# The first batch's keys pooled by matmuls place by place, two rows of inverse sums made by TensorE, and w_out's column scale from sums of magnitudes

## The chip, the cores and the metric

The kernel runs on one core of one Trainium2 chip. The metric is the device time of one execution in microseconds, taken as the median of several. "Before" is the kernel as it stands, "the change" the kernel with the edits below. Besides the five engines (TensorE, VectorE, ScalarE, GpSimd, SyncE; in the profile PE, DVE, ACT, POOL, SP) the core has 16 DMA engines, here fed from SyncE's queue alone.

## What is computed

```python
B, S, C, F = 4, 12288, 128, 2048
kv_pool = kv.reshape(B, 96, 4, 8, 4, C).mean(axis=(2, 4))      # 768 keys a batch, 16 places each
k = v = kv_pool.reshape(B, 768, C) @ w_sr
a = softmax(q @ k.T / sqrt(C))
x = (a @ v).reshape(-1, C)
h = x @ w_in
out = (h - tanh(h)) @ w_out
```

Inputs and output are float32, and the weights of the feed-forward come as float64 words. The keys of one batch are sums over 16 places of the input (4 by 4 neighbours), multiplied with w_sr.

## The kernel before

The tokens are cut into 96 groups of 512, 24 a batch. Each group passes through attention and then through the feed-forward, and the two are software-pipelined: while TensorE does the feed-forward of one group, the attention of later groups runs on the other engines.

*Keys of a batch* (`keys`). Twelve loads of 64 keys by 16 places come in (the first batch's last four cut in halves, in buffers borrowed from tiles that are not used yet). VectorE sums the 16 places of each (`pool`, L475), TensorE multiplies with w_sr (`product`, L505), VectorE takes the maximum and makes a power of two of it (`size`, L514 and L455 to L459), and ScalarE and VectorE write the two float16 halves `vt`, high and low (L521, L525); a transposing DMA makes `vv` of it. Then the scale of w_in enters (`shares`, L539), a diagonal is spread over all partitions by a matmul (L263, L266), and the chain L544 to L550 ends the batch's scales in `vs`. q's halves `qh` and `ql` (L608, L611) wait for that.

*Weights.* `weights_in` and `weights_out` build float32 values from the words of the doubles in four pieces each (`words_of`: L302 to L327 on VectorE, L306 on ScalarE, L331 on GpSimd; the words in two buffers). w_in gets one scale (`wis`, L357) and two float16 halves. w_out gets a scale for each of its 128 columns: column maxima of each piece (L396), the maximum of those (L400), a turn by TensorE (L412), a maximum (L416), a power of two, and a second spread; then the pieces are scaled (L427) and cut into halves (`woh`, `wol`), with a scaled-down copy `wos` on GpSimd (L438).

*Attention of a group.* For each of four token tiles: six matmuls of scores (L636) into bank `s` (or `h` early on), negated maximum `nm` (L644, L646), exponentials `e` with their sum (L650), their halves `a` (L655 on ScalarE, L658 on GpSimd), and a transposing DMA into `at` (L662). Then the inverse sums (L675, L676) are stored to DRAM and loaded back as one row on all partitions (L679, L683). 18 matmuls make `x` (L694); the division `xf` multiplies with the row (L707), and two halves of x follow: the high one on ScalarE (L711), the low one on VectorE (L714).

*Feed-forward of a group.* Eight units: six matmuls into `h` (L734 to L736), tanh and square on ScalarE (L762, L765), `gg` on VectorE (L768), `gh` on GpSimd or ScalarE (L772, L776), `gl` on VectorE (L779), six matmuls into `acc` (L740 to L742).

*Order.* Every operation is given to a planner (`Plan.op`) with a step number, an engine, an estimated duration and what it reads and writes. `Plan.run` then runs a list schedule with those numbers and emits the instructions in that order; each engine executes its own in order. A table `SHIFT` moves all operations of one kind by a constant. Buffers of a tag form a ring, and an operation on a tile waits until the tile's previous user in the ring is done.

## Time and profile before

| | before |
|---|---|
| median of three runs | 2895.05 us (2893.52 to 2896.0) |
| the profiled execution, its time | 2894.31 us |
| the profiled execution, its span | 2892.5 us |
| TensorE busy | 2780.9 us, 96% of the span |
| VectorE busy | 2724.7 us, 94% |
| ScalarE busy | 2590.1 us, 90% |
| GpSimd busy | 1377.9 us, 48% |
| mean granted clock of TensorE | 0.994 |

The span runs from the first to the last instruction. An engine's busy time is the union of its instructions. The granted clock is given as a share of 2.4 GHz. In timelines and chains the times are from the start of the span; a row such as "L514" names a line of the kernel before. What stands in brackets behind a row is the idle time of that engine ahead of it, with what ended it.

### The profile page before, as it was taken

What the parts mean: (1) busy time and instruction counts of PE and PEld (TensorE: products, weight loads), DVE (VectorE), ACT (ScalarE), POOL (GpSimd) and SP (SyncE); (2) the same over time, 40 slices, a digit from 0 to 9 for tenths busy, and PEclk for the clock granted to TensorE, in tenths of its full rate; (3) what the DMA queues carried; (4) which work ended last, traced back from release to release, by engine and by line L of the source; (5) the groups of instructions that cost most, each with busy time, mean ns of one, the idle gap of its engine ahead of it and who ended that gap; (6) DMA issues with size and microseconds to landing.
All of it is one profiled execution on the core that took longest, in us unless ns stands there. A gap on an engine that the chain in (4) does not pass through costs nothing.

```text
span 2892.5 us, 39309 instructions
## 1 busy us (share of the span) xinstructions
PE 2780.9 (96%) x13286; PEld 1301.3 (45%) x13286; DVE 2724.7 (94%) x3230; ACT 2590.1 (90%) x3289; POOL 1377.9 (48%) x1073
## 2 busy tenths in 40 slices
PE   2799999999999999999999999999999999999998
PEld 1344444444444444444444444444444444444443
DVE  7899999999999999999999999999999999999997
ACT  3799999998999999998799999999889999999986
POOL 2455454544454545454354445444435454544442
PEclk9899999999999999999999999999999999999999
DMA  6754444676354444477454444457637444444430
GB/s 166 122 94 84 99 84 99 113 150 93 76 106 89 99 92 88 99 133 130 72 104 97 84 102 85 100 99 145 107 70 117 95 88 99 85 99 84 95 83 22
DMA packets 737187, 285.53 MB, mean 99 GB/s; under 512 B 666192, under 2 KB 692944, under 8 KB 736976
## 3 DMA queue, kind: packets, MB, share of 16 engines
q1 hardware_dynamic: 736976, 282.94, 50.5%
q8 instruction: 106, 1.74, 0.4%
q14 instruction: 105, 0.86, 0.2%
HBM read 79.76 MB, written 50.53 MB: 45 GB/s over the span
## 4 chain that ended last, share of the span: by engine, by line
PE 65%; DVE 20%; ACT 6%; issue 4%; DMA 2%; POOL 1%; SPq 0%; DVEq 0%; ACTq 0%; POOLq 0%
PE x L694 9%; PE s L636 9%; PE h L734 8%; PE h L736 8%; PE h L735 8%; PE acc L741 8%; PE acc L740 8%; PE acc L742 8%; DVE gl L779 7%; DVE gg L768 6%; DVE nm L644 3%; ACT t L762 2%; DVE kvp L475 1%; DMA kc<-in_kv_dram 1%; ACT e L650 1%
## 5 line engine op out<-in xcount | busy, mean ns | idle before, releaser
L772 POOL TENSOR_SCALAR gh<-gg 128x1024 f16<-128x1024 f32 x672 | 731.6, 1089 | 1216.6 <-DVE gl L779 659.7
L768 DVE SCALAR_TENSOR_TENSOR gg<-h,by_batch,t 128x1024 f32<-128x1024 f32 x768 | 983.2, 1281 | 81.7 <-ACT t L765 25.4
L779 DVE SCALAR_TENSOR_TENSOR gl<-gh,gg 128x1024 f16<-128x1024 f16 x768 | 1022.1, 1332 | 7.4 <-POOL gh L772 1.7
L762 ACT ACTIVATE t<-h,by_batch 128x1024 f32<-128x1024 f32 x768 | 849.4, 1106 | 130.6 <-PE h L736 130.0
L765 ACT ACTIVATE t<-t 128x1024 f32<-128x1024 f32 x768 | 811.0, 1056 | 21.2
L658 POOL TENSOR_TENSOR a<-e,a 128x768 f16<-128x768 f32 x384 | 631.9, 1646 | 232.3 <-ACT t L765 59.3
L734 PE MATMUL h<-x,wih 128*128 128x512 f16 x1536 | 582.9, 379 | 15.5 <-DVE gg L768 12.6
L742 PE MATMUL acc<-gl,wos 128*128 128x512 f16 x1536 | 582.1, 379 | 1.5 <-DVE gl L779 1.5
L735 PE MATMUL h<-x,wih 128*128 128x512 f16 x1536 | 582.5, 379 | 0.6 <-DVE x L714 0.6
L736 PE MATMUL h<-x,wil 128*128 128x512 f16 x1536 | 582.5, 379 | 0.0
L741 PE MATMUL acc<-gh,wol 128*128 128x512 f16 x1536 | 582.1, 379 | 0.0
L740 PE MATMUL acc<-gh,woh 128*128 128x512 f16 x1536 | 582.1, 379 | 0.0
L694 PE MATMUL x<-at,vv 128*128 128x512 f16 x1728 | 467.9, 380 | 3.3 <-DMA at<-a 3.0
L650 ACT ACTIVATE e<-s,nm 128x768 f32<-128x768 f32 x380 | 339.9, 894 | 65.8 <-DVE nm L646 56.4
L644 DVE TENSOR_REDUCE nm<-s 128x1 f32<-128x768 f32 x380 | 360.9, 950 | 24.3 <-PE s L636 23.7
L636 PE MATMUL s<-vt,qh 128*128 128x384 f16 x1520 | 312.2, 328 | 36.3 <-ACT e L650 33.8
L655 ACT CAST a<-e 128x768 f16<-128x768 f32 x384 | 314.9, 822 | 6.0 <-DMA at<-a 2.4
L694 PEld LDWEIGHTS <-vv 128*128 128x128 f16 x1728 | 169.3, 98 | 206.5 <-issue 7.6
L734 PEld LDWEIGHTS <-wih 128*128 128x128 f16 x1536 | 150.2, 98 | 195.4 <-DVE gg L768 26.9
L636 PEld LDWEIGHTS <-qh 128*128 128x128 f16 x1536 | 151.3, 99 | 183.6 <-issue 47.4
L735 PEld LDWEIGHTS <-wih 128*128 128x128 f16 x1536 | 150.2, 98 | 184.0 <-issue 22.4
L736 PEld LDWEIGHTS <-wil 128*128 128x128 f16 x1536 | 150.2, 98 | 182.6 <-issue 1.6
(126 smaller groups left out, 1746.6 us busy)
## 6 DMA issues: line engine op xcount, KB each, us to landing
qs<-in_q_dram SPq DMA_DIRECT2D x96, 256.0 KB, 2.7
row<-sums_row SPq DMA_DIRECT2D x96, 256.0 KB, 3.8
xs<-x SPq DMA_DIRECT2D x96, 256.0 KB, 2.5
out_dram<-o SPq DMA_DIRECT2D x96, 256.0 KB, 2.3
kc<-in_kv_dram SPq DMA_DIRECT2D x40, 512.0 KB, 6.6
at<-a SPq DMA_TRANSPOSE x384, 4.6
words<-in_moe_w_in_dram SPq DMA_DIRECT2D x4, 512.0 KB, 6.7
words<-in_moe_w_out_dram SPq DMA_DIRECT2D x4, 512.0 KB, 4.7
```

The lines of the kernel that those rows point to most:

```text
L694: PE.matmul(out=plan[x], lhsT=l, rhs=r, start=(n == 0 and k == 0), stop=(n == KT - 1 and k == 2))
L734: PE.matmul(out=h, lhsT=wih[:, fs], rhs=xh, start=True, stop=False)
L735: PE.matmul(out=h, lhsT=wih[:, fs], rhs=xl, start=False, stop=False)
L736: PE.matmul(out=h, lhsT=wil[:, fs], rhs=xh, start=False, stop=True)
L740: PE.matmul(out=acc, lhsT=woh[:, fs], rhs=gh, start=(f == 0), stop=False)
L741: PE.matmul(out=acc, lhsT=wol[:, fs], rhs=gh, start=False, stop=False)
L742: PE.matmul(out=acc, lhsT=wos[:, fs], rhs=gl, start=False, stop=(f == FT - 1))
L762: A.activation(out=plan[t], in_=plan[h], func=AF.Tanh, scale=node)
L765: A.activation(out=plan[t], in_=plan[t], func=AF.Square)
L768: V.scalar_tensor_tensor(out=plan[gg], in0=plan[h], scalar=weight, in1=plan[t], op0=ALU.mult, op1=ALU.mult)
L772: return PL.tensor_scalar(out=plan[gh], in0=plan[gg], scalar1=1.0 / LOW, scalar2=1.0, op0=ALU.mult, op1=ALU.mult)
L779: return V.scalar_tensor_tensor(out=plan[gl], in0=plan[gh], scalar=-LOW, in1=plan[gg], op0=ALU.mult, op1=ALU.add)
```

## The change

- *First batch's keys.* The host lays the first batch of kv out by place: 16 planes of 768 keys. Each plane is loaded (`load_places`, four of them in halves) and multiplied with w_sr at once (`product_of_place`, L507), and TensorE sums the 16 products in PSUM. The 16 reductions on VectorE are gone for that batch. The later batches are as before.
- *Row of inverse sums.* For groups 0 and 1, ScalarE writes four diagonal matrices from the inverse sums (L741), a matmul with ones makes the row on all partitions in bank `x` (L745), and ScalarE copies it (L749). The store to DRAM and the load back are gone for these two groups.
- *w_out's column scale.* ScalarE takes the magnitudes of each piece divided by the number of rows (L407), TensorE adds them over all rows with ones (L412), so that the sum stands on all partitions at once; the power of two is made of 128 columns (L477 to L482). One small turn and a copy give the column form (L433, L437). `wos` is now written by ScalarE (L459).
- *Words.* Four buffers instead of two, and w_in's loads have step numbers of their own.
- *Planner.* New numbers in `SHIFT`, a new table `EARLY` that moves the first four groups and the two weight stages; an operation waits only for the start of its ring predecessor's first user; and the model makes loads wait for stores of rows.

```diff
-        "turn_weights": 3.55, "values": 1.09, "weight_high": 2.38, "weight_low": 0.83,
+        "turn_weights": 2.45, "values": 1.09, "weight_high": 2.38, "weight_low": 1.0,
...
+    EARLY = {"attention 0": -0.5, "attention 1": -1.7, "attention 2": 0.1, "attention 3": 0.3, "weights_in": -1.5, "weights_out": 5.0}
...
-                    need[i].add(self.tiles[t["ring"][t["place"] - 1]]["by"][0][0])
+                    behind[i].add(self.tiles[t["ring"][t["place"] - 1]]["by"][0][0])
...
-                free["dma"] = max(free.get("dma", 0.0), now + us) + dma
+                landed = free.get("rows", 0.0) if dram == "read" else 0.0
+                free["dma"] = max(free.get("dma", 0.0), now + us, landed) + dma
+                if dram == "rows":
+                    free["rows"] = now + us + late
...
-                    r = max(done[j] + (self.HOP if self.ops[j][1] != f else 0.0) for j in need[k])
+                    r = [done[j] + (self.HOP if self.ops[j][1] != f else 0.0) for j in need[k]]
+                    r = max(r + [begun[j] + 0.01 for j in behind[k]])
...
+    first_kv = kv[0].rearrange("c k w -> c (k w)").rearrange("c (w k) -> c w k", w=W)
...
-        sb(words, "words", [P, WN, 2], U32, 2)
+        sb(words, "words", [P, WN, 2], U32, 4)
...
-        plan.op(step - 4, "SP", 0.5, load, (), (words,), late=2.0, dma=1.3)
+        plan.op(load_step, "SP", 0.5, load, (), (words,), late=2.0, dma=1.3, dram="read")
...
+            words_of(step, step - 46 + 3 * n, n, "i", (wa, slice(n * WN, (n + 1) * WN)))
...
-        def largest(n):
-            V.tensor_reduce(out=plan["cols"][:, n], in_=chunk(n).rearrange("p (t c) -> p c t", c=C),
-                            op=ALU.max, axis=AX.X, apply_absolute_value=True)
-
-        def largest_of_all():
-            V.tensor_reduce(out=plan["cols"][:, NW], axis=AX.X, op=ALU.max,
-                            in_=plan["cols"][:, 0:NW].rearrange("p n c -> p c n"))
+        def sizes(n, aw):
+            A.activation(out=plan[aw], in_=chunk(n), func=AF.Abs, scale=1.0 / F)
+
+
+        def sums(n, aw):
+            for t in range(two):
+                PE.matmul(out=plan["sum.o"][:, 0:P], lhsT=ones, rhs=plan[aw][:, t * P : (t + 1) * P],
+                          start=(n == 0 and t == 0), stop=(n == NW - 1 and t == two - 1))
 
         for n in range(NW):
             key, at = places[n]
-            words_of(step + n, n, "o", (key, slice(at, at + WN)))
-            plan.op(step + n, "DVE", 0.67, partial(largest, n), ((key, at),), (("cols", n),))
-        plan.op(step + NW, "DVE", 0.67, largest_of_all, [("cols", n) for n in range(NW)], (("cols", NW),))
+            aw = f"aw.o.{n}"
+            words_of(step + n, step + n - 4, n, "o", (key, slice(at, at + WN)))
+            sb(aw, "aw", [P, WN], F32, 2)
+            plan.op(step + n, "ACT", 0.62, partial(sizes, n, aw), ((key, at),), (aw,), late=0.1)
+            plan.op(step + n, "PE", 1.0, partial(sums, n, aw), (aw, "ident"), ("sum.o",), late=0.2,
+                    wide=True)
+
+        def scale_row():
+            return plan["sum.o"][:, P : 2 * P]
+
+        def power():
+            power_of_two(plan["sum.o"][:, 0:P], plan["col_back"], 2.0**-100, scale_row(), F)
...
-            PE.matmul(out=plan["turned"][:, 0:P], lhsT=plan["cols"][:, NW], rhs=ident, start=True, stop=True)
-
-        def power():
-            by, back = col[:, 1:2], col[:, 0:1]
-            V.tensor_reduce(out=by, in_=plan["turned"][:, 0:P], op=ALU.max, axis=AX.X)
-            power_of_two(by, back, 2.0**-100)
-
-        plan.op(step + NW, "PE", 0.3, turn, (("cols", NW), "ident"), ("turned",), late=0.2, wide=True)
-        plan.op(step + NW, "DVE", 0.8, power, ("turned",), ("col",))
-        bank("scale.o", "acc", 1, 1)
-        spread(step + NW, lambda: col[:, 1:2], "col", "scale.o")
+            PE.matmul(out=plan["turned"][:, 0:1], lhsT=plan["col_back"], rhs=ident[:, 0:1],
+                      start=True, stop=True)
+
+        def copy():
+            V.tensor_scalar(out=col[:, 0:1], in0=plan["turned"][:, 0:1], scalar1=1.0, scalar2=None,
+                            op0=ALU.mult)
...
-            PL.tensor_scalar(out=wos[:, sl], in0=woh[:, sl], scalar1=1.0 / LOW, scalar2=1.0,
-                             op0=ALU.mult, op1=ALU.mult)
+            A.activation(out=wos[:, sl], in_=woh[:, sl], func=AF.Copy, scale=1.0 / LOW)
...
-        pieces = [(n, KB, "kc", 5) for n in range(KN)]
-        if not b:
-
-            half = [(tag, 4) for tag in ("gh", "gl") for _ in range(4)]
-            full = [("t", 2), ("gg", 2), ("kc", 5)] * 2 + [("kc", 5)] * 2
-            pieces = [(n, KB, *full[n]) for n in range(KN - 4)]
-            pieces += [(n, KB // 2, *half[n - 2 * (KN - 4)]) for n in range(2 * (KN - 4), 2 * KN)]
...
+        def load_places(n, c, key):
+            at = slice(0, K) if c is None else slice(c * KH, (c + 1) * KH)
+            SP.dma_start(out=plan[key], in_=first_kv[:, n, at])
+
+
+        def product_of_place(n, cs, keys):
+            for c, key in zip(cs, keys):
+                at = plan[key] if len(cs) == 1 else plan[key][:, c * KH : (c + 1) * KH]
+                PE.matmul(out=plan[pk][:, c * G : c * G + KH], lhsT=wsr, rhs=at, start=(n == 0),
+                          stop=(n == W - 1))
...
+            tags = [("t", 2), ("gg", 2), ("kc", 5)] * 2 + [("kc", 5)] * 3
+            tags += [(("gh", 4), ("gl", 4))] * 4 + [("kc", 5)] * 3
+            for n, tag in enumerate(tags):
+                s = s0 - 40 + n
+                if isinstance(tag[0], tuple):
+                    for c, (name, bufs) in enumerate(tag):
+                        key = f"kc.{b}.{n}.{c}"
+                        sb(key, name, [P, KH], F32, bufs)
+                        plan.op(s + c / 2, "SP", 0.45, partial(load_places, n, c, key), (), (key,),
+                                late=2.0, dma=0.5)
+                        plan.op(s + c / 2, "PE", 0.72, partial(product_of_place, n, (c,), (key,)),
+                                (key,), ((pk, c),), wide=True)
+                else:
+                    key = f"kc.{b}.{n}"
+                    sb(key, tag[0], [P, K], F32, tag[1])
+                    plan.op(s, "SP", 0.45, partial(load_places, n, None, key), (), (key,), late=2.0,
+                            dma=1.0)
+                    plan.op(s, "PE", 1.44, partial(product_of_place, n, (0, 1), (key, key)), (key,),
+                            (pk,), wide=True)
...
+        def diagonals():
+            for t in range(TT):
+                A.activation(out=plan[f"inv_at.{g}"][:, t], in_=ident, func=AF.Copy,
+                             scale=plan[inv][:, t : t + 1])
+
+        def sum_of_rows():
+            PE.matmul(out=plan[f"row_at.{g}"], lhsT=ones,
+                      rhs=plan[f"inv_at.{g}"].rearrange("p t k -> p (t k)"), start=True, stop=True)
+
+        def copy_row():
+            A.copy(out=plan[row], in_=plan[f"row_at.{g}"])
...
-        plan.op(s1, "SP", 0.5, store_row, (inv,), (f"dram.{g}",), late=11.0, dma=0.8)
-        plan.op(s1, "SP", 0.5, load_row, (f"dram.{g}",), (row,), late=5.0, dma=0.65)
+        if g < ROWS:
+            inv_at, row_at = f"inv_at.{g}", f"row_at.{g}"
+            plan.op(s1, "ACT", 1.2, diagonals, (inv, "ident"), (inv_at,), late=0.1)
+            plan.op(s1, "PE", 1.0, sum_of_rows, (inv_at, "ident"), (row_at,), late=0.2, wide=True)
+            plan.op(s1, "ACT", 0.51, copy_row, (row_at,), (row,), late=0.1)
...
-    identity(-LEAD - 8)
-    weights_in(-LEAD - 1)
+    early = Plan.EARLY.get
+    identity(-LEAD - 60)
+    weights_in(-LEAD - 1 + early("weights_in", 0.0))
...
+            attention(g, g * UN - LEAD + early(f"attention {g}", 0.0))
...
+    win[0] = win[0].transpose(0, 2, 1).reshape(win[0].shape)
```

The order in which instructions stand changes with it. On SyncE's queue the loads of w_in's words move to the head (second, fourth, eighth and twelfth in the queue, between the places of the keys), and two loads of q and two of w_out's words stand ahead of the last two places. Three places are shown, each first before, then in the change.

SyncE's queue (`kc` are keys, `words` the weights' words, `qs` queries, `vv` the values) where w_out's words (L290 before, L300 in the change) and the transposes of the scores' weights (L662, L715) meet. Before:

```order
L288 DMA words_155<-in_moe_w_in_dram 128x1024
L288 DMA words_168<-in_moe_w_in_dram 128x1024
L290 DMA words_195<-in_moe_w_out_dram 128x4x256
L530 DMA_TRANSPOSE vv_198<-vt_190 128x12x128
L290 DMA words_211<-in_moe_w_out_dram 128x4x256
L603 DMA qs_258<-in_q_dram 128x512
L662 DMA_TRANSPOSE at_309<-a_286 128x12x128
L662 DMA_TRANSPOSE at_309<-a_301 128x12x128
L679 DMA sums_row_83<-inv_318 128x4x1
L603 DMA qs_346<-in_q_dram 128x512
L662 DMA_TRANSPOSE at_309<-a_313 128x12x128
L662 DMA_TRANSPOSE at_309<-a_321 128x12x128
```

In the change:

```order
L300 DMA words_164<-in_moe_w_out_dram 128x4x256
L300 DMA words_172<-in_moe_w_out_dram 128x4x256
L501 DMA kc_182<-in_kv_dram 128x768
L501 DMA kc_188<-in_kv_dram 128x768
L300 DMA words_196<-in_moe_w_out_dram 128x4x256
L300 DMA words_213<-in_moe_w_out_dram 128x4x256
L578 DMA_TRANSPOSE vv_260<-vt_254 128x12x128
L656 DMA qs_297<-in_q_dram 128x512
L656 DMA qs_317<-in_q_dram 128x512
L715 DMA_TRANSPOSE at_377<-a_349 128x12x128
L715 DMA_TRANSPOSE at_377<-a_365 128x12x128
L715 DMA_TRANSPOSE at_377<-a_374 128x12x128
```

All four loads of w_out's words stand ahead of the first transposes, and the stores of inverse sums are gone from among the transposes of groups 0 and 1.

VectorE around the first division `xf`. Before, from the third piece's column maxima on:

```order
L396 TENSOR_REDUCE cols<-kc 128x128
L302 TENSOR_SCALAR ym<-words 128x512
L644 TENSOR_REDUCE nm<-s 128x1
L646 TENSOR_SCALAR nm<-nm 128x1
L707 SCALAR_TENSOR_TENSOR xf<-x,vs,row 128x512
L309 SCALAR_TENSOR_TENSOR ym<-ym 128x512
L314 TENSOR_SCALAR ym<-ym 128x512
L318 SCALAR_TENSOR_TENSOR kc<-ym 128x512
L323 TENSOR_SCALAR ym<-kc 128x512
L327 SCALAR_TENSOR_TENSOR ym<-words,ym 128x512
L714 TENSOR_TENSOR x_537<-xf,x_537 128x512
L718 TENSOR_REDUCE most_x<-x_537 128x1
```

In the change, from the maximum of the eleventh tile on:

```order
L697 TENSOR_REDUCE nm<-s 128x1
L699 TENSOR_SCALAR nm<-nm 128x1
L781 SCALAR_TENSOR_TENSOR xf<-x,vs,row 128x512
L788 TENSOR_TENSOR x_578<-xf,x_578 128x512
L792 TENSOR_REDUCE most_x<-x_578 128x1
L697 TENSOR_REDUCE nm<-s 128x1
L699 TENSOR_SCALAR nm<-nm 128x1
L477 TENSOR_SCALAR col_back<-acc 128x128
L478 TENSOR_SCALAR acc<-col_back 128x128
L480 TENSOR_SCALAR col_back<-acc 128x128
L482 RECIPROCAL acc<-col_back 128x128
L448 TENSOR_TENSOR o<-o,acc 128x512 x2
```

The fourth piece's decoding (L302 to L327), which needs a load, stood around the division; now the division stands behind a maximum, and w_out's scale follows on 128 columns of the bank `acc`.

ScalarE from the first exponentials on. Before:

```order
L650 ACTIVATE e,sums_all<-s,nm 128x768
L655 CAST a<-e 128x768
L650 ACTIVATE e,sums_all<-h,nm 128x768
L655 CAST a<-e 128x768
L650 ACTIVATE e,sums_all<-h,nm 128x768
L650 ACTIVATE e,sums_all<-s,nm 128x768
L655 CAST a<-e 128x768 x2
L608 ACTIVATE qh<-qs,vs 128x512
L616 ACTIVATE qj,squares<-qs,vs 128x512
L650 ACTIVATE e,sums_all<-s,nm 128x768
L650 ACTIVATE e,sums_all<-h,nm 128x768
L306 ACTIVATE ym<-ym 128x512
```

In the change:

```order
L407 ACTIVATE aw<-o 128x512
L703 ACTIVATE e,sums_all<-s,nm 128x768
L703 ACTIVATE e,sums_all<-h,nm 128x768
L708 CAST a<-e 128x768
L703 ACTIVATE e,sums_all<-h,nm 128x768
L708 CAST a<-e 128x768 x2
L703 ACTIVATE e,sums_all<-s,nm 128x768
L708 CAST a<-e 128x768
L741 ACTIVATE inv_at<-ident,inv 128x128 x4
L661 ACTIVATE qh<-qs,vs 128x512
L703 ACTIVATE e,sums_all<-s,nm 128x768
L749 COPY row<-x 128x512
```

The magnitudes of w_out's pieces (L407), the diagonals (L741) and the row's copy (L749) now stand between the exponentials and casts of the first groups.

## Rows read from the trace of the kernel before

**Rows 1.** Busy time by stretch: length, then engines, granted clock, DMA share and GB/s.

```profile
140.00:2890.00 2750.00, 2712.07 (x13015) 1271.37 (x13012) 2612.35 (x3038) 2517.42 (x3177) 1328.30 (x1032) 1.00 0.50 96
```

**Rows 2.** Timeline of VectorE, 31 to 49 us: start, duration, line, operation.

```profile
32.65 0.96 DVE L514 TENSOR_REDUCE vs<-s 128x1 f32<-128x768 f32 x1
...
37.24 0.42 DVE L302 TENSOR_SCALAR ym<-words 128x512 f32<-128x512 f32 x1
...
40.79 0.69 DVE L327 SCALAR_TENSOR_TENSOR ym<-words,ym 128x512 f32<-128x512 uint32 x1
...
43.69 0.16 DVE L357 TENSOR_REDUCE wis<-top 128x1 f32<-128x4 f32 x1
...
44.44 0.16 DVE L459 RECIPROCAL wis<-wis 128x1 f32<-128x1 f32 x1
44.52 0.20 DVE L539 TENSOR_SCALAR vs<-vs,wis 128x1 f32<-128x1 f32 x1
...
47.01 0.21 DVE L550 TENSOR_SCALAR vs<-vs,by_batch 128x1 f32<-128x1 f32 x1
```

**Rows 3.** Timeline of SyncE's queue, 55 to 100 us.

```profile
60.06 12.76 SPq L662 DMA_TRANSPOSE at<-a  x2
...
80.54 0.42 SPq L290 DMA_DIRECT2D words<-in_moe_w_out_dram  x1
```

**Rows 4.** The page, DMA issues: count, KB each, median us from issue to landing.

```profile
at<-a SPq DMA_TRANSPOSE x384, 4.6
```

**Rows 5.** Chain that ended last, 56 to 116 us: start, duration, what.

```profile
80.54 12.42 DMA words<-in_moe_w_out_dram
...
94.46 0.66 DVE xf L707
...
113.91 1.15 DVE gl L779
```

**Rows 6.** Busy time by stretch, the loads at the start.

```profile
2.00:26.00 24.00, 1.65 (x2) 0.50 (x2) 16.85 (x22) 1.34 (x3) 1.26 (x1) 1.00 0.97 352
```

**Rows 7.** Timeline of TensorE around two products with w_sr: batch 0, then batch 1.

```profile
17.86 1.65 PE L505 MATMUL s<-kvp,wsr 128*128 128x384 f32 x2 [17.86 <-DVE kvp L475]
...
711.68 1.45 PE L505 MATMUL s<-kvp,wsr 128*128 128x384 f32 x4
712.97 0.81 PE L694 MATMUL x<-at,vv 128*128 128x512 f16 x3
```

**Rows 8.** Timeline of TensorE, 46 to 107 us.

```profile
57.03 1.44 PE L636 MATMUL s<-vt,qh 128*128 128x384 f16 x4 [2.42 <-ACT e L650]
...
60.49 0.81 PE L636 MATMUL h<-vt,qh 128*128 128x384 f16 x4
...
86.14 0.81 PE L636 MATMUL s<-vt,qh 128*128 128x384 f16 x4 [2.45 <-ACT e L650]
...
98.75 0.59 PE L735 MATMUL h<-x,wih 128*128 128x512 f16 x1 [0.62 <-DVE x L714]
```

**Rows 9.** Groups of ScalarE by shape, 47 to 98 us: count, busy us, mean ns, idle before.

```profile
L655 ACT CAST a<-e 128x768 f16<-128x768 f32 x11 | 9.0, 826 | 2.6 <-DMA at<-a 2.4
L650 ACT ACTIVATE e<-s,nm 128x768 f32<-128x768 f32 x8 | 7.2, 898 | 6.1 <-DVE nm L646 5.9 <-POOL a L658 0.2
...
L608 ACT ACTIVATE qh<-qs,vs 128x512 f16<-128x512 f32 x5 | 3.6, 712 | 3.7 <-DMA qs<-in_q_dram 3.7
...
L306 ACT ACTIVATE ym<-ym 128x512 f32<-128x512 f32 x3 | 1.9, 629 | 7.8 <-DVE ym L302 7.8
...
L616 ACT ACTIVATION_READ_ACCUMULATOR qj<-qs,vs 128x1 f32 x5 | 0.9, 188 | 0.0
```

**Rows 10.** Groups of VectorE by shape, 0 to 104 us: same columns.

```profile
L396 DVE TENSOR_REDUCE cols<-kc 128x128 f32<-128x512 f32 x2 | 2.1, 1034 | 0.3 <-POOL kc L331 0.3
...
L676 DVE RECIPROCAL inv<-inv 128x4 f32<-128x4 f32 x3 | 0.5, 178 | 0.1
...
L263 DVE TENSOR_SCALAR d<-ident,vs 128x128 f32<-128x128 f32 x1 | 0.3, 288 | 0.0
```

More of the change, by code (lines that the diff above doesn't have):

```diff
@@ L109, in op @@
         step += self.SHIFT.get(kind, 0.0)
-        self.ops.append((step, engine, us, emit, late, port or engine == "POOL", dma, wide))
+        self.ops.append((step, engine, us, emit, late, port or engine == "POOL", dma, wide,
+                         dram))
         self.names[name] = i
@@ L120, in run @@
         n = len(self.ops)
-        need = [set() for _ in range(n)]
+        need, behind = [set() for _ in range(n)], [set() for _ in range(n)]
         for i, name in self.later:
@@ L132, in run @@
                 if t["place"]:
-                    need[i].add(self.tiles[t["ring"][t["place"] - 1]]["by"][0][0])
+                    behind[i].add(self.tiles[t["ring"][t["place"] - 1]]["by"][0][0])
         then = [[] for _ in range(n)]
-        left = [len(s) for s in need]
-        for i, s in enumerate(need):
-            for k in s:
+        left = [len(need[i] | behind[i]) for i in range(n)]
+        for i in range(n):
+            for k in need[i] | behind[i]:
                 then[k].append(i)
-        free, ready, done, order, was_wide = {}, {}, [0.0] * n, [], True
+        free, ready, done, begun, order, was_wide = {}, {}, [0.0] * n, [0.0] * n, [], True
         for i in range(n):
@@ L166, in run @@
                 free["port"] = now + us
-            done[i] = now + us + late
+            begun[i], done[i] = now, now + us + late
             order.append((now, i))
@@ L385, in weights_out @@
         sb("wb.2", "kc", [P, 2 * WN], F32, 5)
[L386 removed]
+        sb("col_back", "col_back", [P, P], F32, 1)
+        bank("sum.o", "acc", 1, 1)
         plan.tile("col", "col", 1, lambda: None)
@@ L424, in scaled @@
+        plan.op(step + NW, "DVE", 0.8, power, ("sum.o",), ("sum.o", "col_back"))
+        plan.op(step + NW + 4, "PE", 0.1, turn, ("col_back", "ident"), ("turned",), late=0.2,
+                wide=True)
+        plan.op(step + NW + 4, "DVE", 0.1, copy, ("turned",), ("col",))
         def scaled(n):
-            row = plan["scale.o"][:, 0:P].unsqueeze(1).to_broadcast([P, two, P])
+            row = scale_row().unsqueeze(1).to_broadcast([P, two, P])
             y = chunk(n).rearrange("p (t c) -> p t c", c=C)
@@ L904, in attention_any @@
         sums = halves(pk)[:, :, 0:KH]
-        vs, vt = t("vs", [P, 3]), t("vt", [P, 2, K], F16)
-        back, by = vs[:, 0:1], vs[:, 1:2]
-        V.tensor_reduce(out=by, in_=sums, op=ALU.max, axis=AX.XY, apply_absolute_value=True)
-        power_of_two(by, back, 2.0**-80)
-        keys = kvp
+        vt = t("vt", [P, 2, K], F16)
+        keys, by = kvp, by_batch[:, b, 7:8]
         A.activation(out=halves(keys), in_=sums, func=AF.Copy, scale=scale / W)
```

97 lines of the change are left out of this document (58 added, 39 removed).

## The prediction

> **What bounds the kernel now.** I read the busy time by stretch first. From 140 us to 2890 us TensorE is busy for 2712.1 of 2750 us at a granted clock of 1.00, and VectorE for 2612 [rows 1]. All that TensorE waits there comes to 37.9 us. Anything that only lightens another engine there buys next to nothing. So what is left to win lies in the head, and I asked what delays the first matmuls of the feed-forward: I read the chain of waits, then the timelines, from there back.
>
> The reader should see four dates in the head. (1) The maximum over the first batch's projected keys starts at 32.65, but the step that needs it together with w_in's scale, L539, starts at 44.52, because the scale itself begins only at 43.69 [rows 2]. The first scores need that chain's L550 at 47.01; I call its end S (47.2 before). (2) The queue of DMAs on SyncE then sits for most of 12.76 us on two transposes, and issues the last load of w_out's words only at 80.54 [rows 3]. (3) That load takes 12.42 us, and VectorE, which runs in order, stands at it; only then, at 94.46, comes the division xf of group 0, whose row is long there [rows 5]. (4) The first projection gets its second operand x at 98.75 [rows 8]; call this F. The first gl, which opens the back projection, begins at 113.91 and ends at 115.1 [rows 5].
>
> **The change, part by part.** My method: find S, F and the end of the first gl anew; what the last gains, the end gains, because from there on TensorE's work per group is the same and it is full.
>
> *T, the end of the pooled product.* It is now 16 places of two f32 matmuls with 384 columns each. Each is two passes. Warm, four passes take 712.97 - 711.68 = 1.29 us a place; cold, two took 1.65 us, which fits passes at half the clock, 0.64 each and 2.56 a place [rows 7]. The loads ahead of the last place are 16 x 0.393 MB of keys, 4 x 0.524 of w_in, 2 x 0.524 of w_out, 2 x 0.262 of q, in all 9.96 MB (sizes from the shapes in the order of SyncE's queue). From 2 to 26 us the loads ran at 352 GB/s [rows 6], which gives 28.3 us, from 2.2 to 30.5. The last place adds 1.29 to 2.56. I take T = 32.5, with bounds 30 and 35 (another 8% of rate either way).
>
> Whether TensorE keeps up depends on its clock. Row: after an idle of 2.42 us four score matmuls took 1.44 us at 57.03, and after 3.5 us of unbroken work 0.81 us at 60.49 (the clock went from 1.2 to 2.4 GHz); at 86.14, after a wait of 2.45 us that followed a fuller stretch, they still took 0.81 [rows 8]. In the change the first places cost 2.56 us cold while one lands about every 1.3 us, so TensorE falls behind, works unbroken, and should rise to 2.4 GHz by the fourth or fifth place; then 1.29 a place is as fast as the loads. The Trainium skill ("TensorE: Matmul & The Clock Gate", section "Loop structure matters more than you think") says the opposite of a loop in which every matmul waits for a DMA: the engine goes back to the low clock. By that rule every place would cost its cold price, and the sum would be rival A's, below.
>
> *S.* w_in's decode no longer shares VectorE with the pooling (8 reductions of 1024 columns and 8 of 512 are gone) and its loads are in front. One piece took from 37.24 to 41.48, 4.24 us [rows 2]; four from the first landing at 3.9 end at 21, and with POOL's add, the last maximum and the scale, 3 us, at 24. So L539's successor waits for T alone, even behind four wil (3 us) and a top that waits for w_out's words at about 28. After T: maximum and six small steps 2.1 us, two decode steps queued between 1.1, the low half of vt 1.0, the share, the diagonal, the matmul 1.3, the chain to L550 1.3 (before, 44.52 to 47.22 for the last two). S = T + 6.8 = 39.3, 7.9 us earlier.
>
> *S to F.* No load of w_out is left behind the transposes, and groups 0 and 1 get their row from TensorE, so neither the load's 12.42 us nor a DRAM trip is in the way. What is left is ScalarE's queue up to x_high, which I count in the new order: 11 exps of 0.90 + 0.19 for the accumulator = 11.9, 9 casts of 0.83 = 7.5, 4 qh 2.8, 5 qj of 0.90 = 4.5, 4 sizes of w_out and 2 ym at 0.63 = 3.8 [rows 9], and x_high 0.6. New: 8 diagonals of 128 columns; no such row, so between 0.19 (one column) and 0.63 (512), near 0.30 by the line between them: 2.4; one row copy, as a 512-column step, 0.6. Sum 34.1 us. On top come waits: the first maximum behind two ql and two decode steps (1.2), the next groups' turns of the score bank (about 0.6 each, four times), and the tenth exp, whose scores stand behind nine x matmuls on TensorE (2 to 4); the second row's matmul, in x's bank, can only come after xf and stands ahead of the first projection (1). x itself needs the fourth transpose. The first goes out about 10 us after S, behind two exps, a cast and GpSimd's half; a transpose takes 4.6 us to land in the median [rows 4], so the last of four lands between S + 20, if they overlap, and S + 28, if they don't: before ScalarE gets that far. With xf, x_high, x_low I get F = S + 42 (bounds: S + 35 without any wait, S + 45). F = 81.3, against 98.7.
>
> *F to the first gl.* Gone are a column maximum and the overall one (1.03 each, 2.1 [rows 10]), one ql (0.7) and the chain on one column (1.3). New is the chain on 128 columns in PSUM: three steps of 0.29 and a reciprocal. No row has it; 0.29 is the floor, and 4 columns cost 0.178 against 0.16 for one [rows 2, 10], so 6 ns a column and 0.9 for 128; I take 0.9, 1.8 for the chain. A second xf comes in (0.7), a copy (0.15). 16.4 becomes 15.1. w_out's scaled-down copies move from POOL to ScalarE, 4 x 0.6; they lie between two tanh steps there, and VectorE needs its 11 us for the weights in that stretch anyway, so I cost them at nothing; bare, 2.4.
>
> *Less work in hand.* At the first gl the new order has 13 score tiles read instead of 14: 1.0 us of TensorE, 1.1 of VectorE, 1.9 of ScalarE, still to do. I take 1.4.
>
> *The rest of the run.* The numbers that set the order are new, and buffers now wait only for their predecessor's start. Some steps swap places in each group, no instruction is added from group 2 on. What TensorE waits is 37.9 us in the whole stretch [rows 1], so the gain is at most that; a loss has no such bound, and I allow 8 us either way and take zero.
>
> **Sum.** 7.9 + 9.5 + 1.3 - 1.4 = 17.3 us off. The profiled execution took 2894.31 (span 2892.5), 0.74 below the median of the three runs, so 2877.0 for it and 2877.5 for a median: 0.6% faster.
>
> **The rivals.**
> A. *TensorE stays at 1.2 GHz through the places.* 16 x 2.56 = 41 us from the first landing at 5.0: T = 46, S = 52.8, F = 94.8, first gl 109.9 instead of 115.1, and 1.4 of that lost to the work in hand: 2890.5. For it: at 57.03 a wait of 2.4 us was enough to fall. Against it: 86.14, and that the cold engine cannot be short of places. This is the case that the Trainium skill's rule would give.
> B. *The transposes set the head's pace.* SyncE's queue stands 12.76 us on two transposes before, 10 more than they take it elsewhere [rows 3], and nothing in the change makes a transpose cheaper. One such stand on group 0's four puts the last at S + 34; x's 18 matmuls (7 us at the low clock) and the 3 us behind them put F at S + 44, inside the forecast's range. Two put it at S + 54 and cost 12 of the 17 us: 2889. For it: they now come four and four without a pause. Against: the long stand comes right behind the store of the inverse sums in many small pieces, and this store is gone for two groups.
> C. *The new order costs a wait in every group.* Place: the score bank or gg, for which TensorE waits in the long stretch. The other 92 groups pay it each time: at 0.19 us a group the 17.3 us are gone, at 0.25 it is slower by 0.2%; at 0.3, 2905. For it: VectorE is at 95% of that stretch [rows 1], with little room. Against: no work is added there.
> D. *The new order also saves waits there.* A third of the 37.9 us, with the head as forecast: 2865.
>
> **How the numbers follow.** Forecast (17.3 us off, its own range 2867 to 2886 from T's 2.5, F's 3 to 7 and the rest's 8, which partly cancel) 0.76; A 0.05; B 0.06; C 0.04; D 0.09. The range 2864 to 2888 holds the forecast's case but for its tails and more than half of D, 0.8 in all, and leaves A, B and C out. About 0.2% (5.8 us) is what a measurement can tell from no change: faster means below 2889.3. The forecast, D and a third of A and B make 0.89; the rest of A and B 0.07; C 0.04.
>
> **What would show it.** Right: the f32 matmuls of the places at 1.29 us by the middle of the loads and done at 30 to 35; first scores near 40; no wait of VectorE for w_out's words; ScalarE close to full from S to F; first projection at 78 to 85; first gl near 96; from there to the end the same time as before within 8 us. Wrong: places at 2.56 us to the last (A); TensorE waiting for transposes at the first x (B); a stretch from 140 us on in which TensorE's busy share falls below 98.6% (C).

## The result, and the profile after

The changed kernel takes 2870.52 us (median of four runs, 2869.81 to 2871.49), the kernel before 2894.87 beside it. The ratio is 0.9916, 95% interval 0.9899 to 0.9933: 24.4 us faster, with 19 to 29 inside the interval. Forecast were 17.3 us and 2877.5, range 2864 to 2888. The profiled execution took 2871.49 us, its span 2869.8: 22.7 less than before.

Busy time by stretch, first the long stretch of the changed kernel, which answers to [rows 1], then both kernels cut at 200 us (each pair stands under its own kernel):

```profile
core 0: us, PE busy (x) PEld busy (x) DVE busy (x) ACT busy (x) POOL busy (x), PEclk, DMA share, GB/s
140.00:2870.00 2730.00, 2691.16 (x12927) 1263.55 (x12925) 2586.84 (x3023) 2498.90 (x3157) 1327.12 (x1027) 1.00 0.51 97
0.00:200.00 200.00, 170.14 (x738) 83.67 (x738) 172.23 (x253) 152.80 (x223) 87.42 (x67) 0.92 0.55 135
200.00:2900.00 2700.00, 2631.84 (x12644) 1236.03 (x12642) 2528.74 (x2960) 2442.55 (x3085) 1294.64 (x1003) 1.00 0.51 96
```

The kernel before:

```profile
0.00:200.00 200.00, 128.36 (x559) 57.93 (x560) 169.65 (x255) 129.94 (x185) 82.21 (x65) 0.92 0.65 129
200.00:2900.00 2700.00, 2652.51 (x12728) 1243.39 (x12726) 2555.05 (x2976) 2460.13 (x3105) 1295.68 (x1008) 1.00 0.50 96
```

TensorE waits 38.8 us in its long stretch (2730 less 2691.2), as against 37.9 before. The gain lies ahead of it: at 200 us TensorE has 20.7 us less work left (2652.5 less 2631.8). It idled 29.9 us up to there instead of 71.6; the other half of those 41.8 us is work that the change gives to TensorE, the pooling above all (its matmuls are busy for 23.6 us, those of the product before for 3.3). Behind 200 us it idles 2.0 us less: together the 22.7.

Timeline of TensorE, the product place by place (it answers to [rows 7]):

```profile
7.35 2.90 PE L507 MATMUL s<-t,wsr 128*128 128x384 f32 x4 [7.35 <-DMA t<-in_kv_dram]
...
12.44 1.45 PE L507 MATMUL s<-kc,wsr 128*128 128x384 f32 x4
13.73 1.45 PE L507 MATMUL s<-t,wsr 128*128 128x384 f32 x4
...
29.81 2.85 PE L507 MATMUL s<-kc,wsr 128*128 128x384 f32 x8 [1.73 <-DMA kc<-in_kv_dram]
```

From the third place on the starts are 1.29 us apart; the first two stand 2.69 and 2.40 us apart. Timeline of VectorE from w_in's scale to the end of the first scale's chain (to [rows 2]):

```profile
25.69 0.16 DVE L482 RECIPROCAL wis<-wis 128x1 f32<-128x1 f32 x1
27.34 0.43 DVE L312 TENSOR_SCALAR ym<-words 128x512 f32<-128x512 f32 x1 [1.48 <-DMA words<-in_moe_w_out_dram]
...
32.70 0.96 DVE L562 TENSOR_REDUCE vs<-s 128x1 f32<-128x768 f32 x1 [0.21 <-PE s L507]
...
39.29 0.21 DVE L598 TENSOR_SCALAR vs<-vs,by_batch 128x1 f32<-128x1 f32 x1
```

w_in's scale is there at 25.9 instead of 44.6, and the maximum at 32.70 waits for the product alone (the waits for w_out's words at 27.34 and 28.81, of 1.48 and 1.04 us, lie ahead of the product's end). SyncE's queue, and the page's row of the transposes (to [rows 3, 4]):

```profile
49.14 7.19 SPq L715 DMA_TRANSPOSE at<-a  x4
...
62.13 11.07 SPq L715 DMA_TRANSPOSE at<-a  x4
...
at<-a SPq DMA_TRANSPOSE x384, 4.1
```

No load of words is left behind the transposes. Then TensorE at the first projection (to [rows 8]), VectorE and ScalarE up to the first gl (to [rows 5, 10]):

```profile
81.39 0.38 PE L809 MATMUL h<-x,wih 128*128 128x512 f16 x1
```

```profile
82.43 0.29 DVE L480 TENSOR_SCALAR col_back<-acc 128x128 f32<-128x128 f32 x1
82.75 0.96 DVE L482 RECIPROCAL acc<-col_back 128x128 f32<-128x128 f32 x1
...
88.86 0.66 DVE L455 TENSOR_TENSOR wol<-kc,woh 128x512 f16<-128x512 f32 x1
89.44 0.95 DVE L697 TENSOR_REDUCE nm<-s 128x1 f32<-128x768 f32 x1
...
90.50 1.28 DVE L842 SCALAR_TENSOR_TENSOR gg<-h,by_batch,t 128x1024 f32<-128x1024 f32 x1
...
93.53 1.22 DVE L853 SCALAR_TENSOR_TENSOR gl<-gh,gg 128x1024 f16<-128x1024 f16 x1
```

```profile
82.85 1.10 ACT L836 ACTIVATE t<-h,by_batch 128x1024 f32<-128x1024 f32 x1
84.47 0.62 ACT L451 CAST woh<-o 128x512 f16<-128x512 f32 x1 [0.51 <-DVE o L448]
85.12 0.63 ACT L459 ACTIVATE wos<-woh 128x512 f16<-128x512 f16 x1
...
88.63 0.63 ACT L459 ACTIVATE wos<-woh 128x512 f16<-128x512 f16 x1
89.17 1.04 ACT L839 ACTIVATE t<-t 128x1024 f32<-128x1024 f32 x1
```

Between projection and first gl, VectorE and ScalarE are splitting w_out: the first square (L839) stands from 83.96 to 89.17 behind eight copies of w_out, and the first gg on VectorE behind the low halves (wol). This is the place to keep in mind.

Four dates are used below: S and F as in the prediction, W, the end of w_out's last low half, and O, the end of the first gl that comes with or after W. W, and O in place of the first gl's end, are no dates of the prediction; they were chosen with the runs in hand. In all runs but e4, O is the end of the first gl.

### The profile page after: what moved, and what is told of

It is laid out like the page before. It is cut to its first block, busy times and chain, and to the rows that moved or that the text cites. A ratio compares the mean times of both kernels' runs of the same rounds, so it can differ in the third digit from the quotient of the medians.

```text
span 2869.8 us, 39539 instructions
## 1 busy us (share of the span) xinstructions
PE 2802.0 (98%) x13380; PEld 1319.7 (46%) x13380; DVE 2701.0 (94%) x3212; ACT 2595.3 (90%) x3307; POOL 1382.1 (48%) x1069
## 4 chain that ended last, share of the span: by engine, by line
PE 70%; DVE 19%; ACT 5%; issue 3%; DMA 1%; POOL 1%; DVEq 0%; SPq 0%; ACTq 0%; POOLq 0%
PE x L768 9%; PE s L689 9%; PE h L808 9%; PE h L810 9%; PE h L809 9%; PE acc L815 8%; PE acc L814 8%; PE acc L816 8%; DVE gl L853 6%; DVE gg L842 6%; DVE nm L697 3%; ACT t L836 2%; DVE kvp L496 1%; ACT e L703 1%; ACT a L708 1%
## 5 line engine op out<-in xcount | busy, mean ns | idle before, releaser
L839 ACT ACTIVATE t<-t 128x1024 f32<-128x1024 f32 x768 | 810.9, 1056 | 20.7
L816 PEld LDWEIGHTS <-wos 128*128 128x128 f16 x1536 | 150.3, 98 | 181.1
```

Of the source, the lines that this page charges most:

```text
L816: PE.matmul(out=acc, lhsT=wos[:, fs], rhs=gl, start=False, stop=(f == FT - 1))
L839: A.activation(out=plan[t], in_=plan[t], func=AF.Square)
```

## The experiments

All dates are of the profiled execution, in us. "Before" ran beside each set; its median was 2892.2 for e1 to e4, 2895.0 for e0, e5, e6 and e8, 2895.5 for e9, e11 and e12, 2896.3 for e13, so kernels of different sets are compared by the ratio. The span is that of one execution. The two can differ by several us: beside e1 to e4 the kernel before was 2.7 us faster than beside the first measurement, and the changed kernel did not run in that set.

| | median | ratio (95%) | S | F | W | O | span |
|---|---|---|---|---|---|---|---|
| before | 2894.87 | 1 | 47.2 | 98.8 | 113.9 | 115.1 | 2892.5 |
| changed | 2870.52 | 0.9916 (0.9899 to 0.9933) | 39.5 | 81.4 | 89.5 | 94.8 | 2869.8 |
| e0 changed again | 2870.78 | 0.9918 (0.9904 to 0.9931) | 39.3 | 80.6 | 88.7 | 94.0 | 2868.4 |
| e1 pooling on VectorE | 2880.57 | 0.9958 (0.9944 to 0.9972) | 46.6 | 86.4 | 100.0 | 104.1 | 2879.4 |
| e2 rows by DRAM | 2876.37 | 0.9945 (0.9931 to 0.9958) | 40.0 | 90.6 | 92.0 | 99.0 | 2874.5 |
| e3 column maxima | 2873.49 | 0.9937 (0.9923 to 0.9950) | 40.7 | 79.5 | 96.6 | 97.8 | 2871.7 |
| e4 words in two buffers | 2875.51 | 0.9941 (0.9927 to 0.9954) | 38.4 | 76.8 | 100.7 | 101.8 | 2873.6 |
| e5 old order | 2871.07 | 0.9918 (0.9904 to 0.9931) | 46.1 | 85.1 | 82.2 | 95.6 | 2870.3 |
| e6 new order alone | 2891.82 | 0.9989 (0.9980 to 0.9998) | 49.0 | 108.2 | 118.0 | 123.7 | 2893.4 |
| e8 x earlier | 2874.76 | 0.9930 (0.9916 to 0.9943) | 39.7 | 77.9 | 90.6 | 96.2 | 2873.1 |
| e9 low halves on GpSimd | 2872.10 | 0.9917 (0.9904 to 0.9931) | 39.3 | 79.0 | 87.4 | 92.4 | 2868.8 |
| e11 lower part three times | 2875.99 | 0.9932 (0.9918 to 0.9945) | 40.6 | 85.9 | 94.0 | 99.2 | 2874.3 |
| e12 e9 and top on GpSimd | 2874.66 | 0.9927 (0.9913 to 0.9940) | 41.4 | 80.2 | 87.6 | 95.3 | 2872.4 |
| e13 e9 in the old place | 2869.99 | 0.9912 (0.9899 to 0.9926) | 39.1 | 78.9 | 87.3 | 92.3 | 2865.2 |

**e0**, the changed kernel as it is.

> The changed kernel itself, as it is, beside the other runs of this set and the same runs of the kernel before. If the difference between chips is a factor for both kernels, the ratio is 0.9916 again (0.9899 to 0.9933).

The ratio came again.

**e1.** The pooling goes back to VectorE:

```diff
...
-                    plan.op(s, "PE", 1.44, partial(product_of_place, n, (0, 1), (key, key)), (key,),
-                            (pk,), wide=True)
...
+                plan.op(s, "DVE", 1.13 * size / KB, partial(pool, n, size, 0, key), (key,),
+                        ((kvp, (j, 0)),))
...
```

> Only the first part of the change is undone: the first batch's keys are pooled by VectorE again, in the old layout and the old 12 pieces, with one product behind them; rows of inverse sums, w_out's scale and the new order rules stay. The theory (what is won at the end of the first scale's chain is handed on whole to the end): that chain ends some 7.7 us later, near 47.2 as before the change instead of 39.5, the first projection gets its second operand near 89 instead of 81.4, and the time is 2878 us (2876 to 2880). The rival (the head behind that chain has slack, since ScalarE stands idle for 12.7 of the 39.4 us there and the x group stands 14 us in TensorE's order behind transposes that landed): under 3 us come back, 2871 to 2873.5.

About 10 us come back (9.6 by the span, 10.1 by the medians, 12 by the ratio): the theory's side, half a us above its range, and more than S's 7.1. But F comes only 5.0 later, and O 9.3: the shift did not travel along the dates as foretold.

**e2.** `ROWS = 2` becomes `ROWS = 0`.

> Only the second part is undone: the row of inverse sums of the first two groups goes by DRAM again, as it does for all others. The theory (the two stands of SP of 11.1 and 10.4 us, which went away, were what the head's second half waited for): the first transposes land some 8 to 10 us after their issue again, and the time is near 2880 us (2877 to 2883). The rival (that wait was covered: x is multiplied only 14 us after the transposes landed, so a row that is 10 us later and transposes that queue behind it change nothing): 2870.5 to 2872.5, with the first projection's second operand within 2 us of 81.4.

Between the two: 4.7 us by the span, 8 by the ratio. F is 9.2 later, and O only 4.2: half of F's delay is covered. TensorE and VectorE of e2:

```profile
90.61 0.63 PE L809 MATMUL h<-x,wih 128*128 128x512 f16 x1
```

```profile
91.27 0.76 DVE L455 TENSOR_TENSOR wol<-kc,woh 128x512 f16<-128x512 f32 x1
94.46 1.28 DVE L842 SCALAR_TENSOR_TENSOR gg<-h,by_batch,t 128x1024 f32<-128x1024 f32 x1 [2.43 <-ACT t L839]
...
97.75 1.22 DVE L853 SCALAR_TENSOR_TENSOR gl<-gh,gg 128x1024 f16<-128x1024 f16 x1
```

With w_out's last low half done 1.4 us behind F, F to O takes 8.4 us. In the changed kernel, where it is done 8.1 us behind F, it takes 13.4.

**e3.** The column maxima return:

```diff
...
-            plan.op(step + n, "ACT", 0.62, partial(sizes, n, aw), ((key, at),), (aw,), late=0.1)
-            plan.op(step + n, "PE", 1.0, partial(sums, n, aw), (aw, "ident"), ("sum.o",), late=0.2,
-                    wide=True)
...
+            plan.op(step + n, "DVE", 0.67, partial(largest, n), ((key, at),), (("cols", n),))
...
```

> Only the third part is undone: w_out's column scale comes from column maxima on VectorE again (five reductions of about 1.04 us, a transposing product, a spread row), while the words keep four buffers and the small copy of w_out stays on ScalarE. The theory (VectorE's work lies on the way from the first scale to the first projection): 3 us slower, 2872.5 to 2875. The rival (w_out's chain has time until the second product of the feed-forward needs it, 13 us behind the first projection's operand, and VectorE is idle between): within 1 us of the changed kernel, 2870 to 2871.5.

Span +1.9, medians +3.0, ratio +0.0021 (6 us) with intervals that overlap: the theory's 3 us lie in between, but they are not certain. F is 1.9 earlier, W 7.1 later, O 3.0 later.

**e4.** The words' four buffers become two.

> The words of the two weights get two buffers again instead of four; all else is the changed kernel. The theory (four buffers let w_out's words be loaded ahead, which takes the 12.4 us wait for words at 80.5 of the kernel before away): that load comes late again and the time is 2875 to 2880 us. The rival (with two buffers the loads still start before the first batch's softmax, since the order of the plan has moved ahead too): 2870.5 to 2872.5.

3.8 us slower by the span, 5 by the medians and 7 by the ratio, though F comes 4.6 us earlier: the time that the theory named. The first projection went ahead, and a first gl ended at 84.7, 7.9 us behind F; then VectorE was still unpacking w_out (this timeline is of e4):

```profile
82.03 0.52 DVE L312 TENSOR_SCALAR ym<-words 128x512 f32<-128x512 f32 x1
...
83.49 1.22 DVE L853 SCALAR_TENSOR_TENSOR gl<-gh,gg 128x1024 f16<-128x1024 f16 x1 [0.66 <-POOL gh L846]
...
100.03 0.68 DVE L455 TENSOR_TENSOR wol<-kc,woh 128x512 f16<-128x512 f32 x1
100.63 1.22 DVE L853 SCALAR_TENSOR_TENSOR gl<-gh,gg 128x1024 f16<-128x1024 f16 x1
```

**e5 and e6**, order and edits apart. e5 has the three edits, the words' four buffers and the old order, e6 the old work, two buffers and the new order. Table and early steps of e5 are shown; the planner's rules go back with them:

```diff
     SHIFT = {
-        "divide": 1.11, "exps": -0.64, "forth": 0.46, "fro": 3.89, "g_high": 1.39, "g_low": 0.59,
+        "divide": 0.59, "exps": -0.64, "forth": 0.46, "fro": 3.72, "g_high": 1.39, "g_low": 0.59,
...
-    EARLY = {"attention 0": -0.5, "attention 1": -1.7, "attention 2": 0.1, "attention 3": 0.3, "weights_in": -1.5, "weights_out": 5.0}
+    EARLY = {}
```

> All three edits of the work stay, and the order is made by the old rules: the old table of shifts, no early steps, the old edges between the tiles of a ring, no wait of loads behind the store of a row. The theory (the edits bring the gain and the new rules only some 5 us, what the three single undoings of 9, 5 and 2 us and the buffers' 4 us leave of 24): 5 us above the changed kernel, ratio to before 0.992 to 0.995. The rival (the head's order depends on the early steps, the old rules put the attention of the first groups late): 10 us or more above the changed kernel, ratio 0.995 or more.

> The counterpart: the kernel before with none of the three edits and two buffers for the words, but its order made by the new table, early steps and rules. The theory (the rules alone bring little, since what the head waits for is VectorE's pooling and the row by DRAM): within 5 us of the kernel before, ratio 0.998 to 1.002. The rival (a good part of the 24 us is order): 8 us or more faster, ratio 0.997 or less.

e6 is 3 us faster than before by the medians, as its theory allowed; its trace is that of the slowest of its eleven executions (2895.09). e5 refutes both of its own: with the ratio of e0 beside it, it costs nothing. And it does so with S 6.6 us later than in the changed kernel, near its date before the change. VectorE of e5, and its first projection on TensorE:

```profile
39.35 0.95 DVE L561 TENSOR_REDUCE vs<-s 128x1 f32<-128x768 f32 x1
...
45.89 0.21 DVE L597 TENSOR_SCALAR vs<-vs,by_batch 128x1 f32<-128x1 f32 x1
...
81.47 0.68 DVE L454 TENSOR_TENSOR wol<-kc,woh 128x512 f16<-128x512 f32 x1
...
93.37 2.19 DVE L852 SCALAR_TENSOR_TENSOR gl<-gh,gg 128x1024 f16<-128x1024 f16 x1
```

```profile
85.07 0.38 PE L808 MATMUL h<-x,wih 128*128 128x512 f16 x1 [0.70 <-DVE x L787]
```

The old order unpacks part of w_out ahead of S. So F is 3.7 later, W 7.4 earlier, and O 0.8 later: what the scale lost, w_out won.

**e8.** x's matmuls earlier:

```diff
-            plan.op(at_step + 1.0, "SP", 1.6, turn_weights, (a,), ((at, t),), late=3.5, dma=3.3)
+            plan.op(at_step + 1.0, "SP", 1.6, turn_weights, (a,), ((at, t),),
+                    late=2.3 if g == 0 else 3.5, dma=0.5 if g == 0 else 3.3)
```

> The changed kernel, but the planner takes the transposes of the first group to land after 2.3 us with 0.5 us of queue for each, instead of 3.5 and 3.3, near the 3.6 to 4.1 us seen; so TensorE multiplies that group's x behind the fifth scores instead of behind the ninth. The theory (the x group stood 14 us in the order and not for data, and TensorE idles 5.7 us between 60 and 70): the first projection has its second operand 8 to 10 us earlier, and 3 to 6 us come off the time, ratio 0.9895 to 0.9905. The rival (as with two buffers for the words, where that operand was 4 us earlier and the time 4 us longer: what follows is held by the later groups and by TensorE's sum of work and waits): 0 to 4 us more than the changed kernel, ratio 0.9916 to 0.993.

The run came out on the rival's side. x starts at 58.7 instead of 72.4 and F is 3.5 us earlier, but the span is 3.3 us longer (the ratio is 0.0012 above that of e0 beside it, with intervals that overlap). VectorE of e8:

```profile
89.87 0.68 DVE L455 TENSOR_TENSOR wol<-kc,woh 128x512 f16<-128x512 f32 x1
90.47 1.28 DVE L843 SCALAR_TENSOR_TENSOR gg<-h,by_batch,t 128x1024 f32<-128x1024 f32 x1
...
94.98 1.23 DVE L854 SCALAR_TENSOR_TENSOR gl<-gh,gg 128x1024 f16<-128x1024 f16 x1
```

The first gg stands behind w_out's low halves as in the changed kernel, W is 1.0 later, O 1.5.

**e9, e12, e13**, on a new theory, that VectorE's sum of work sets the head. e9 and e13 give GpSimd the same four steps; in e9 the planner knows it, in e13 it does not, so that TensorE, ScalarE and SyncE keep the changed kernel's order; e12 moves w_out's first step too. This is the whole edit of e13, and a part of the other two:

```diff
-            V.tensor_tensor(out=wol[:, sl], in0=chunk(n), in1=woh[:, sl], op=ALU.subtract)
+            PL.tensor_tensor(out=wol[:, sl], in0=chunk(n), in1=woh[:, sl], op=ALU.subtract)
```

> The changed kernel, but the four low halves of w_out (0.68 us of VectorE each) are made by GpSimd, planned at 1.2 us each; nothing ahead of the first scale is touched. The new theory (what counts in the head is VectorE's sum of work up to the first groups, since it stands about 25 us in every kernel so far and the date of the eighth gl follows its work): 2.7 us of VectorE's work less, 2 to 3 us off the time, ratio 0.9905 to 0.991. The rival (only TensorE's waits behind the scale count, and these four have cover): the time of the changed kernel, ratio 0.9915 to 0.992; if GpSimd delivers later than VectorE did, more.

> As the run with w_out's low halves on GpSimd, and the first step of w_out's words (four minima and maxima of 0.42 us) on GpSimd too. The new theory: 4.4 us of VectorE's work less than in the changed kernel, 3 to 4.5 us off the time, ratio 0.990 to 0.9905, the fastest kernel so far. The rival (GpSimd shares its way to memory with VectorE's and has the low halves of the first group's weights to make between 47 and 54, so w_out's words come late behind it): 0 to 4 us more than the changed kernel.

> The changed kernel with every engine in its own order; only the four low halves of w_out are given to GpSimd where VectorE had them, so 2.7 us less of VectorE's work stand between the first projection and the first gl, and nothing else moves. If VectorE's sum of work alone sets the head: the first gl ends 2 to 2.7 us earlier, near 92.3, and the time is 2 to 2.5 us less, ratio 0.9907 to 0.991. The rival (there ScalarE holds the chain: the first square stood from 83.96 to 89.17 behind eight of ScalarE's copies of w_out, which stay; the earlier run with these halves on GpSimd had 13.0 us from the second operand to the first gl, as the changed kernel, and won its 2.4 us ahead of it by another order): first gl within 0.8 us of 94.75, the time of the changed kernel, ratio 0.9913 to 0.992.

e9 is the changed kernel's time again, e12 three us above it, both on the rivals' side; e9's interval still holds its theory's ratio, e12's does not. e13's ratio lies between its two forecasts, and its profiled execution was the fastest of five (2866.94; median 2869.99). Its first gl ends at 92.3, the date that its theory named. But F is 2.5 us earlier as well, ahead of the four steps that were moved, and F to O is 13.4 us, as in the changed kernel, though VectorE no longer makes the halves. The same holds of e9 (F 2.4 earlier, F to O 13.4). TensorE, ScalarE and VectorE of e13:

```profile
78.90 0.38 PE L809 MATMUL h<-x,wih 128*128 128x512 f16 x1
```

```profile
86.14 0.63 ACT L459 ACTIVATE wos<-woh 128x512 f16<-128x512 f16 x1
86.68 1.04 ACT L839 ACTIVATE t<-t 128x1024 f32<-128x1024 f32 x1
```

```profile
87.75 1.28 DVE L842 SCALAR_TENSOR_TENSOR gg<-h,by_batch,t 128x1024 f32<-128x1024 f32 x1 [1.17 <-ACT t L839]
...
91.04 1.22 DVE L853 SCALAR_TENSOR_TENSOR gl<-gh,gg 128x1024 f16<-128x1024 f16 x1
```

VectorE now waits at the first gg for the square, and the square still stands behind ScalarE's copies. Lightening VectorE alone won nothing there.

**e11.** For each of w_out's chunks:

```diff
-            V.scalar_tensor_tensor(out=m(), in0=plan[words][:, :, 0], scalar=2.0**-52, in1=y(),
-                                   op0=ALU.mult, op1=ALU.mult)
+            for _ in range(3 if kind == "o" else 1):
+                V.scalar_tensor_tensor(out=m(), in0=plan[words][:, :, 0], scalar=2.0**-52, in1=y(),
+                                       op0=ALU.mult, op1=ALU.mult)
```

> The changed kernel in the same order, but for each of w_out's four chunks of words VectorE makes the lower part three times instead of once (eight operations of 0.7 to 0.9 us more, 5.5 to 7 us in all, into the same place). They lie behind the end of the first scale's chain and ahead of the first gl, where VectorE is idle for some 11 of 40 us, and w_out is needed last there. The new theory (VectorE's sum of work): 4 to 7 us more, ratio 0.993 to 0.994. The rival (VectorE's idle time between the scale and the first projection takes them): under 1.5 us, ratio 0.9915 to 0.9922, with the first projection's second operand within 1 us of 81.4.

The eight steps, of 0.693 us in the median, are 5.5 us of work. Two of them stand ahead of S, which comes 1.1 later; W and O come 4.5 later, the span is 4.5 longer, the ratio 0.0014 to 0.0016 higher. VectorE's idle time ahead of F did not take them, and F moved 4.5 as well, which the rival excluded. The theory's number came, and work added to VectorE there counts almost in full. Whether it does so on the way to F or to W, e11 does not tell. Taken away behind F, where ScalarE holds the next step, VectorE's work won nothing (e13).

## Why the forecast held, and which step of it did not

**The dates.** T (32.7 against 32.5), S (39.5 against 39.3) and F (81.4 against 81.3) came as worked out, and so did the price without a row: the reciprocal of 128 columns at 0.96 (0.9 taken), its chain at 1.9 (1.8). Rival A is refuted by the 1.29 us of the places, which hold on behind the 1.73 us wait for the load at 29.81. The durations decide this: the granted clock reads 1.00 from the start up to 36 us, over the two slow places as well. From 8 to 28 us TensorE has no pause, and only the first place and the one at 29.81 show a wait for a load. The Trainium skill ("TensorE: Matmul & The Clock Gate", section "Loop structure matters more than you think") gives the low clock to a loop with a long DMA wait between every matmul; this loop was not one, so the trace does not test the rule, and rival A was not its case. Rival B is refuted for the changed kernel: group 0's transposes land 3.9 to 4.1 us after their issue and x starts 14 us after the last. C and D are both out by the 38.8 us of waits, against 37.9. The busy share that was to be C's sign, 98.6%, stood too near that of before to tell anything: it was 98.62% and is 98.58%.

**The terms.** S gave 7.7 us (7.9 foretold) and S to F 9.6 (9.5). F to O gave 3.0 instead of 1.3. What follows O gave 2.4 instead of taking 1.4: less work in hand and the rest, which I had put at -1.4 and 0, were mis-sized by 3.8 us together. These differences make the 5.4 us between 17.3 and 22.7. Of the rest, 2.0 us are TensorE's idle time behind 200 us; which steps saved them stays open.

**ScalarE from S to F.** The sum of 34.1 us came out at the right date for the wrong reason. ScalarE is busy 13.9 and 13.6 of 20 us there, not close to full (fourth column of busy times):

```profile
40.00:60.00 20.00, 14.85 (x59) 8.08 (x60) 15.18 (x28) 13.90 (x29) 8.32 (x5) 0.67 0.52 106
60.00:80.00 20.00, 13.94 (x57) 7.78 (x57) 13.30 (x23) 13.55 (x28) 11.69 (x7) 0.66 0.55 112
```

From S to the start of x_high at 78.88 ScalarE is busy for 26.7 us. Of the 34.1 us, some qh and qj, 3 us, ran ahead of S, and in the rows a step that follows at once starts some 0.1 us before the one ahead of it ends, which I had not counted. In place of my 8 us of waits I find 12.7. That the two errors cancel is luck. What I read now is a round trip through one score buffer. TensorE, VectorE, ScalarE, changed kernel:

```profile
68.78 1.44 PE L689 MATMUL s<-vt,qh 128*128 128x384 f16 x4 [2.34 <-ACT e L703]
70.01 0.84 PE L689 MATMUL s<-vt,ql 128*128 128x384 f16 x2
```

```profile
70.89 0.96 DVE L697 TENSOR_REDUCE nm<-s 128x1 f32<-128x768 f32 x1 [2.60 <-PE s L689]
```

```profile
67.74 0.90 ACT L703 ACTIVATE e<-s,nm 128x768 f32<-128x768 f32 x1 [0.99 <-POOL kc L341]
...
72.16 0.90 ACT L703 ACTIVATE e<-s,nm 128x768 f32<-128x768 f32 x1 [1.48 <-DVE nm L699]
```

Scores wait for the exp, the maximum for the scores, the exp for the maximum; the exps at 67.74 and 72.16 are 4.4 us apart. No run changed the number of score buffers, so this is read, not shown.

**The chain.** The step that fell is the method: "find S, F and the end of the first gl anew; what the last gains, the end gains". Its second half held within 6 us: in thirteen of the fourteen traces of the table the end of the span follows O by 2771.7 to 2777.5 us, and by 2769.7 in e6. It needs O for that: in e4 the first gl itself ends 10 us earlier than in the changed kernel, and the span is longer. The first half, by which the first gl follows S and F, came out right, as I read it, only because the other chain moved as well. I had w_out's scaled-down copies on ScalarE at nothing between F and O, and VectorE's work for w_out as a given of 11 us. The traces show two ways that meet at O: x's (S, F, then 7.9 us at the least, in e4 to its first gl, and 8.4 in e2) and w_out's (W, then 1.1 us at the least, e3, e4 and before). The chain that ended last, kernel before (it ends the four low halves at 113.91):

```profile
110.84 3.07 DVE wol L434 x4
```

There W is what ends last, 1.1 us ahead of O, held up by the load at 80.54: VectorE waits for it until 92.98 and is then busy for 21.6 of the 22.1 us to O. In the changed kernel both are close (F and 7.9 is 89.3, W and 1.1 is 90.6), and O stands some 4 us behind the later of the two. So F 3.5 us earlier with W 1.0 later puts O 1.5 later (e8); F 4.6 earlier with W 11.2 later, 7.0 later (e4); S 6.6 and F 3.7 later with W 7.4 earlier, 0.8 later (e5); F 9.2 and W 2.5 later, 4.2 later (e2); F and W both 4.5 later, 4.5 later (e11). On this reading, made after the runs, the change gained because it brought both forward, F by 17.4 and W by 24.4. In the gaps from W to O that lie between 4 and 7.6 us, I take the two engines' order of copies, maxima and gg to decide; how much of it could be saved stays open, since e13 freed one engine and not the other. Four kernels (e5, e9, e13 and the changed one) are alike within what can be measured; none is clearly faster.

**The parts.** Undone singly, the pooling is worth 9.6 us by the spans, the rows 4.7, the buffers 3.8 and the column scale 1.9, 20.0 of 22.7. By the ratios they are 12, 8, 7 and 6 us, together 34 of 24, so the shares are rough and that they add up is not shown. The new order is worth nothing beside the edits (e5) and 3 us by the medians without them (e6).

## What to carry to other kernels

Ahead of the point from which the busiest engine is full, look for every chain that ends there, not only the one on which the profile's chain of waits lies: the others can become the bound as soon as that one is shortened. Moving one date then tells nothing; measure each chain's end beside the date at which the long stretch opens, and check that the end of the run follows that date. A piece of work taken off an engine counts only if no other engine holds the same step for as long.
